# Sums of blocks for a seven-product layer: from subtractions on VectorE to additions in place, a part of them by adding DMA transfers

## The chip, the core and the metric

One core of a Trainium2 chip runs the whole program in one launch. The metric is device microseconds (us) of one execution; lower is better. The kernel before the change takes 979.97 us, the median of three runs (979.74 to 980.07).

## What is computed

Three layers follow one another: an attention whose weights are sigmoids, a two-matrix layer with `h * cos(h)` between its matrices (layer 1), and a two-matrix layer with a rational function between its matrices (layer 2).

```python
scores = scale * q @ k.T - log(S);  attn = 1 / (1 + exp(-scores));  x = attn @ v     # 4 x 12 heads, S = 448, D = 64
h = x @ w_in;  g = h * cos(h);  x = g @ w_out                                       # layer 1: 768 -> 2048 -> 768
h = x @ w_in2                                                                       # layer 2: 768 -> 2048 -> 768
P = a0 + a1*h + a2*h**2 + a3*h**3
Q = 1 + |b0|*|h| + |b1|*h**2
out = (P / (Q + 1e-6)) @ w_out2                                                     # 1792 tokens in all
```

## The kernel before

Every operand of layers 1 and 2 is split into two f16 halves (high and low), and a product is three matmuls: high by high, high by low, low by high. A split is two instructions: ScalarE writes the high half, VectorE subtracts it from the value and writes the low half.

Tokens come in four blocks of 448. Layer 2 takes them in two pairs (`pr` 0 and 1) and treats each of its two matrix products as a 2x2 block product with seven block products in place of eight (`NOP = 7`). For this it needs sums of blocks of the weights (made once, during layer 1) and sums of blocks of the activations (made for each pair), and it adds up the seven results in groups. The stages of layer 2, each once per pair:

- `y_nodes` (L1272) makes the seven activation operands of the first matrix, for each of three row groups `d`: four sums by `sub` (L1313 to 1319, VectorE, f32, 128x448), then the seven splits by `hl` (L1321). It begins when the largest value of layer 1's result is known (`sc`). For pair 1 the sums `t1`, `t2`, `t4` lie in new tiles and the three groups `d` run one after another (`gate`).
- `h2_nodes` (L1477) runs the first matrix: eight steps `k`, each with seven products of nine matmuls, in the order 0, 4, 5, 1, 6, 2, 3. Two PSUM tiles of two banks each, `xv` and `yw`, hold the results. Three small steps pass results between the banks: `seed` (L1513) and `save` (L1517) on ScalarE, and two additions of 128x448 on VectorE, `va` and `wa` (L1520). In each step `va` comes between products 1 and 6 and writes `xv`; `wa` follows product 6 and writes `yw`; product 2 follows `va`, product 3 follows `wa`.
- `item_nodes` (L1435) applies the rational function to the `xv` tile once product 2 is done and to the `yw` tile once product 3 is done: six VectorE instructions of 128x896 each (L110 and L1464) and five on ScalarE (L1449). The first product of the next step waits until the `xv` tile has been read for the last time (`xfree`), the seed until the `yw` tile has (`yfree`).
- `operand_nodes` (L1547) makes the seven operands of the second matrix for each of eight `k`: five sums (L1570 and L1585, VectorE, f32, 128x448) and seven splits (L1554, L1558). The splits are kept in one order over all products and `k` (`order_split`): product 0 for all `k`, then 5, 4, 2, 6, 3, 1.
- `o2_nodes` (L1594) runs the second matrix: seven products, each 24 units of three matmuls (eight `k`, three column groups `e`), and `end` (L1668) takes the banks out: a scaled copy on ScalarE (L1684) or a scaled addition on VectorE (L110, `wt<-o,ig,wt`), then the DMA to the output.

TensorE's order of stages is: first matrix of pair 0 (from about 528 us), the products 0, 5, 4, 2 of pair 0's second matrix (from 674.5 us), the first matrix of pair 1 (from 731.6 us) and then all seven products of pair 1's second matrix (from 875.6 us). Work of another stage is put between the products of a first matrix as filler: 96 units of layer 1 in pair 0, the 72 units of products 6, 3, 1 of pair 0's second matrix in pair 1. `FLOOR0` and `FLOOR1` say how many filler units must have run at each step.

The order on every engine is fixed when the program is built. `arrange` (L688) is a planner: each node has an engine, a duration and dependences, `LAT` holds the delays between engines, and the planner places one instruction after another; a filler unit is taken when the next product isn't ready in the plan. Each engine then runs its instructions in that order. GpSimd takes a few of the sums (`flex`). No DMA is issued from GpSimd; all but two come from SyncE's queue.

Of the kernel before, what the change touches and what calls it, by code (L numbers as in the profile page):

```python
# [10 lines left out]
F32 = mybir.dt.float32  # L11
# [12 lines left out]
def sigmoid_attention_moe_cos_moe_rational(  # L24
# [229 lines left out]
    with tc.manual_schedule():  # L254
# [336 lines left out]
        def l1_consts(bt):  # L591
            i = L1[bt][2]
            ck, iy = (col(f"{n}{bt}", tag=n, bufs=B) for n in ("ck", "iy"))
            ts(V, ck, i, 1.0 / (2.0 * math.pi))
            V.tensor_tensor(out=iy, in0=i, in1=irho, op=ALU.mult)
            return ck, iy
# [28 lines left out]
        g2s, n2s, rgs, wss, obs = (Slots("b", []) for _ in range(5))  # L625
# [18 lines left out]
        class Node:  # L644

            def __init__(self, eng, dur, fn, deps=(), acq=None, rel=None, due=None, soon=False, rush=False, lk=False, cov=False):
                self.eng, self.dur, self.fn = eng, dur, fn
                self.lk, self.cov, self.tied, self.flex, self.patience = lk, cov, False, False, PATIENT
# [11 lines left out]
        SOON, LAG, DMA, AHEAD, ALONE, PATIENT, LATER = 0.3, 0.5, 330.0, 8.0, 3.0, 4.0, 10.0  # L660
# [3 lines left out]
        def lat(a_, b_):  # L664
            return 0.0 if a_ in b_.weak else LAT.get((a_.eng, b_.eng), 0.1)
# [13 lines left out]

        kind = {"V": V.engine, "G": G.engine}  # L680
# [3 lines left out]

# [4 lines left out]
        def arrange(stock, groups, start):  # L689
            nominal = {}  # L690
            t = start
            for k, n in enumerate(pe):
                nominal[n] = t
                t += n.dur
                for g in groups:
                    if g["a"] <= k < g["b"]:
                        at = sorted(g["floors"].items()) + [(g["b"], len(g["units"]))]
                        i = max(i for i, (x, _) in enumerate(at) if x <= k)
                        (x0, n0), (x1, n1) = at[i:i + 2]
                        for u in g["units"][n0 + (n1 - n0) * (k - x0) // (x1 - x0):n0 + (n1 - n0) * (k + 1 - x0) // (x1 - x0)]:  # L700
                            t += u.dur
                            nominal[u] = t
# [63 lines left out]
            def commit(n, t):  # L766
# [3 lines left out]
                if n.lk or n.eng == "G":  # L770
# [13 lines left out]
            while len(queue) < total:  # L784
# [7 lines left out]
                if not cand:  # L792
# [3 lines left out]
                    for g, gr in enumerate(groups):  # L796
                        u = gr["units"]
                        if not u or pos < gr["a"]:
# [19 lines left out]
                for e in ("A", "V", "G", "D"):  # L818
# [3 lines left out]
                    if e == "G":  # L822
                        c = [(max(r, port[0], min(late[n] - ALONE, r + n.patience)), n) for r, n in c]
# [18 lines left out]
                if n.cov and now["G"] <= t + 0.05 and port[0] <= t + 0.05:  # L842
                    c = [m for m in avail["G"] + [m for m in avail["V"] if m.flex and m is not n] for r in (when(m),) if r is not None and r <= t + 0.3]
# [173 lines left out]
        def o1_end(bt, e, unit):  # L1017
            st = {}

            def copy():  # L1020
                r = st[0] = U([P, S], F32, f"yr{bt}_{e}")
                A.activation(out=r, in_=acc1[bt, e][:, :S], func=AF.Copy, scale=L1c[bt][1])
# [72 lines left out]
        s2i, i2i = col("s2i", NDH), col("i2i", ND)  # L1095
        s2o, i2o = (col(n, NFH) for n in ("s2o", "i2o"))
# [37 lines left out]
        def w2i_value_nodes(dues):  # L1134
# [20 lines left out]
            def fin():  # L1155
# [3 lines left out]
                V.tensor_copy(i2i[:, NDH:], i2i[:, :NDH])  # L1159

            scaled["i"] = N("V", 1.3, fin, ends, due=due)

        def w2i_nodes(dues, opened):
            done = []
            for n, (c0, w) in enumerate(W_S):
                stored_in[n] = []
                for rp in range(NDH):
# [19 lines left out]
                    def hl(x, op, deps, free=False, v=v, w=w, rp=rp, n=n, nm=nm, due=due):  # L1187
                        r = hl_nodes(
                            lambda: v[x], w, s2i[:, rp:rp + 1], ws_in[n][:, :, rp, op], [*deps, scaled["i"]],
# [20 lines left out]
        def w2o_nodes(dues):  # L1210
# [3 lines left out]
            for k in range(NFH):  # L1214
# [12 lines left out]
                def fin(k=k, c=c):  # L1227
                    m = col(f"m2p{k}", tag="mro", bufs=2)
                    V.tensor_tensor(out=m, in0=m2o[:, 2 * k:2 * k + 1], in1=m2o[:, 2 * k + 1:2 * k + 2], op=ALU.add)
                    sum_scale(m, s2o[:, c], i2o[:, c], f"2o{k}")  # L1230

# [13 lines left out]
                def hl(get, w, dst, deps, name, free=None, c=c, k=k, fn=fn, due=due):  # L1245
                    r = hl_nodes(
                        get, w, s2o[:, c], dst, [fn, *deps], f"h2o_{k}_{name}", "hl", hs,
# [6 lines left out]
                s1 = tt((2, 0), (0, 1), (1, 1), ALU.add, v3, {"v": 1})  # L1254
# [3 lines left out]
                hb = hl(lambda st=st: st[1]["v"], DM, ws_out[:, 2:4, k], [s1], "b")  # L1258
# [16 lines left out]
        def y_nodes(pr, tmp, drop, res, due, after=()):  # L1275
# [31 lines left out]
            for d in range(NDH):  # L1307
# [5 lines left out]
                def sub(o, i0, i1, deps, new, d=d, b=b, begin=begin, gate=gate):  # L1313
                    def f():
                        if not b:
                            begin()
                        if o not in b:
                            b[o] = tmp([P, S], f"yt{o}_{pr}_{d}")
                        V.tensor_tensor(out=b[o], in0=b[i0], in1=b[i1], op=ALU.subtract)  # L1319
                    return N("V", C448, f, [*gate, *deps], {res: 1} if new else {}, due=due, lk=True)  # L1320

                def hl(x, op, deps, rel, last_users=(), d=d, b=b, begin=begin, gate=gate):
# [6 lines left out]
                    def lo():  # L1329
                        t = tt2[pr, d, op]  # L1330
                        stt(V, t[:, 1, :], b[x], L2[pr][3][:, d:d + 1], t[:, 0, :], ALU.mult, ALU.subtract)
                        if rel and isinstance(x, int):
                            h_, i_ = ((0, 0), (1, 0), (1, 1), (0, 1))[x]
                            SU.drop(f"yr{b0 + i_}_{d + h_ * NDH}")
                        elif rel:
                            drop(f"yt{x}_{pr}_{d}")

                    h = N("A", A448 + PTR, hi, [*gate, *deps], {"u": 1}, due=due)
                    l = N("V", C448 + PTR, lo, [h, *last_users], rel=rel, due=due, lk=True)
                    tt_ready[pr, d, op] = l  # L1340
                    outs.append(l)
                    return h, l

                u1, r1 = {"u": 1}, {res: 1}
                t1 = sub("t1", 3, 0, [], True)
                hl(0, 0, [], u1, [t1])
                t3 = sub(3, 2, 3, [t1], False)
                hl(3, 6, [t3], u1)
                t2 = sub("t2", 2, "t1", [t1], True)
                hl(2, 2, [], u1, [t2, t3])  # L1350
                t4 = sub("t4", 1, "t2", [t2], True)
                hl(1, 1, [], u1, [t4])
                hl("t1", 4, [t1], r1, [t2])
                hl("t2", 5, [t2], r1, [t4])
                gate = [hl("t4", 3, [t4], r1)[1]]
# [46 lines left out]
        def l2_scale(pr):  # L1402
# [11 lines left out]
            ks = []  # L1414
            for n, x in enumerate((L2c[pr][1], ab[:, 2:3], ab[:, 1:2], L2c[pr][2])):
                ks.append(col(f"ks{n}{pr}", NFH))
# [430 lines left out]
```

## Time and profile before

| | |
|---|---|
| median of three runs | 979.97 us |
| profiled execution, own time | 979.13 us |
| its span, first to last instruction | 977.3 us |
| TensorE busy | 960.8 us (98%) |
| VectorE busy | 839.3 us (86%) |
| ScalarE busy | 612.9 us (63%) |
| GpSimd busy | 83.5 us (9%) |
| granted TensorE clock | 1.00 |
| share of the chain that ended last | PE 86%, DVE 12% |

The profile calls TensorE's matmuls PE, VectorE DVE, ScalarE ACT, GpSimd POOL and SyncE SP. Busy time is a mean over stages. A row of a timeline has the start, the length, the engine, the line, the operation, the tiles, and in brackets how long the engine was idle before it and which instruction ended that.

### The profile page before, as it was taken

The numbers are of one execution on the slowest core, as the hardware profiler recorded it, in microseconds if no ns is written. First come the engines' busy times: TensorE is split into PE (matmuls) and PEld (weight loads), VectorE is DVE, ScalarE is ACT, GpSimd is POOL, SyncE is SP. The second block draws the span as 40 slices with busy tenths as digits, with TensorE's granted clock in tenths as the row PEclk, the third lists the DMA queues.
The fourth block names the chain that finished last, engine by engine and source line by source line (L and its number), as shares of the span: only waits on it lengthen the run. The fifth ranks groups of instructions, "written<-read, shape, count | busy, mean of one in ns | idle before, by whom it ended". The sixth has DMA issues, their size and how long they took to land.

```text
span 977.3 us, 14073 instructions
## 1 busy us (share of the span) xinstructions
PE 960.8 (98%) x5255; PEld 486.8 (50%) x5255; DVE 839.3 (86%) x1282; ACT 612.9 (63%) x851; POOL 83.5 (9%) x85
## 2 busy tenths in 40 slices
PE   9999999999999999999999999999999999989998
PEld 4444445555555555555555555555454455444554
DVE  6999979999999879969995698888999999999901
ACT  7999976645755455645774576567685666567600
POOL 0000001220222011210222000001000001000000
PEclk9999999999999999999999999999999999999999
DMA  8788874446455766569612133122343334403353
GB/s 316 275 293 309 306 278 147 168 170 235 162 198 196 245 219 212 201 206 297 213 44 113 57 107 144 57 80 107 112 123 109 122 115 175 134 0 97 114 171 104
DMA packets 70964, 164.50 MB, mean 168 GB/s; under 512 B 6000, under 2 KB 44016, under 8 KB 68848
## 3 DMA queue, kind: packets, MB, share of 16 engines
q1 hardware_dynamic: 70608, 163.26, 49.4%
q8 instruction: 41, 0.67, 0.3%
q10 hardware_dynamic: 288, 0.34, 0.1%
q14 instruction: 27, 0.22, 0.1%
HBM read 129.76 MB, written 33.82 MB: 167 GB/s over the span
## 4 chain that ended last, share of the span: by engine, by line
PE 86%; DVE 12%; issue 1%; ACT 1%; DMA 0%; DVEq 0%; ACTq 0%
PE hx L584 22%; PE o L999 22%; PE o L1645 10%; PE xv L1429 10%; PE v L333 7%; PE yw L1429 7%; PE s L312 5%; DVE ua L1558 2%; DVE ba L110 2%; DVE ba L1570 1%; DVE w L110 1%; DVE ua L110 1%; PE s_None L307 1%; DVE rg L1558 1%; DVE ua L1319 1%
## 5 line engine op out<-in xcount | busy, mean ns | idle before, releaser
L999 PE MATMUL o<-ba,wo 128*128 128x448 f16 x1152 | 226.3, 352 | 0.0
L584 PE MATMUL hx<-ua,wi 128*128 128x448 f16 x1152 | 222.3, 352 | 0.0
L584 PEld LDWEIGHTS <-wi 128*128 128x128 f16 x1152 | 112.5, 98 | 106.1 <-issue 1.4
L999 PEld LDWEIGHTS <-wo 128*128 128x128 f16 x1152 | 112.6, 98 | 105.0
L1429 PEld LDWEIGHTS <-wi 128*128 128x128 f16 x1008 | 98.5, 98 | 99.0 <-issue 7.5
L1645 PEld LDWEIGHTS <-wt 128*128 128x128 f16 x1008 | 98.6, 98 | 98.1 <-issue 6.7
L1645 PE MATMUL o<-ua,wt 128*128 128x448 f16 x630 | 125.7, 352 | 3.0 <-ACT ua L1554 1.5
L1429 PE MATMUL xv<-ua,wi 128*128 128x448 f16 x576 | 117.0, 352 | 2.8 <-DVE ba L110 2.8
L958 POOL TENSOR_TENSOR ba<-ba 128x448 f16<-128x448 f32 x64 | 71.3, 1118 | 458.1 <-DVE ba L107 170.5
L1429 PE MATMUL yw<-ua,wi 128*128 128x448 f16 x432 | 89.5, 352 | 3.2 <-DVE xv L1520 2.1
L110 DVE SCALAR_TENSOR_TENSOR w<-w,u 128x896 f32<-128x896 f32 x64 | 69.0, 1087 | 14.7 <-ACT u L1449 14.1
L317 ACT ACTIVATE a<-s,nlogs 128x896 f32<-128x896 f32 x72 | 69.7, 1013 | 9.1 <-PE s L312 8.9
L110 DVE SCALAR_TENSOR_TENSOR ba<-ua,ba 128x768 int32<-128x768 int32 (+1 forms) x68 | 65.6, 971 | 0.2
L333 PE MATMUL v<-a,v 128*64 128x448 f32 x288 | 63.9, 554 | 0.0
L955 ACT ACTIVATE ba<-ba 128x896 f16<-128x896 f32 x32 | 30.4, 950 | 30.2 <-DVE ba L110 29.8
L1645 PE MATMUL o<-rg,wt 128*128 128x448 f16 x216 | 46.8, 352 | 2.2 <-ACT rg L1554 1.6
L944 ACT ACTIVATE ba<-ba,halfpi 128x896 f32<-128x896 f32 x32 | 33.3, 1040 | 23.1 <-DVE ba L110 22.6
L1449 ACT ACTIVATE ba<-xv,ks,ks 128x896 f32<-128x896 f32 x16 | 17.5, 1096 | 46.9 <-PE xv L1429 46.9
L110 DVE SCALAR_TENSOR_TENSOR wt<-o,ig,wt 128x448 f32<-128x448 f32 (+1 forms) x19 | 12.1, 655 | 40.4 <-PE o L1645 40.4
L1449 ACT ACTIVATE u<-w,c 128x896 f32<-128x896 f32 x32 | 33.2, 1037 | 19.4 <-DVE w L1464 19.4
L110 DVE SCALAR_TENSOR_TENSOR ba<-hx,ck,ba 128x896 f32<-128x896 f32 (+1 forms) x33 | 36.8, 1115 | 9.1 <-ACT ba L937 9.1
L937 ACT ACTIVATE ba<-hx,quarter,ck 128x896 int32<-128x896 f32 (+1 forms) x33 | 35.2, 1066 | 12.2 <-PE hx L584 12.1
(189 smaller groups left out, 1388.4 us busy)
## 6 DMA issues: line engine op xcount, KB each, us to landing
wi<-wsi SPq DMA_DIRECT2D x16, 1344.0 KB, 5.6
wt<-wso SPq DMA_DIRECT2D x56, 384.0 KB, 3.1
ua<-in_moe_w_out_dram SPq DMA_DIRECT2D x21, 768.0 KB, 4.2
p1o<-in_moe_w_out_dram SPq DMA_DIRECT2D x16, 768.0 KB, 6.0
wsi<-ua SPq DMA_DIRECT2D x42, 256.0 KB, 2.9
f1i<-in_moe_w_in_dram SPq DMA_DIRECT2D x12, 768.0 KB, 4.8
wso<-ba SPq DMA_DIRECT2D x24, 384.0 KB, 2.6
ba<-in_moe_w_out_dram SPq DMA_DIRECT2D x11, 768.0 KB, 4.3
```

The costliest lines, as they stand in the source:

```text
L110: eng.scalar_tensor_tensor(out=o, in0=i0, scalar=s, in1=i1, op0=op0, op1=op1)
L312: T.matmul(ps[:, h, :S], mqk[p, "k"][kl][r, c * P:c * P + P], mqk[p, "q"][ql][r], start=(i == 0), stop=(i == 2),)
L317: A.activation(out=t, in_=ps[:, :, :S], func=AF.Sigmoid, bias=cst["nlogs"], scale=QK)
L333: T.matmul(pvt[2 * o + j][h * D:(h + 1) * D, :S], vt[r, b * D:(b + 1) * D], at[r, h], start=c == (None if i else 0), stop=c == (NC - 1 if ...
L584: T.matmul(ps[:, :S], w[:, wl, f * P:(f + 1) * P], x[:, xl, :], start=(n == 0), stop=(n == 3 * ND - 1),)
L937: A.activation(out=o, in_=x, func=AF.Identity, scale=L1c[bt][0], bias=cst["quarter"])
L944: A.activation(out=st["r"], in_=st["r"], func=AF.Sin, scale=2.0 * math.pi, bias=cst["halfpi"])
L958: G.tensor_tensor(out=st["g"][:, j, 1, :], in0=st["r"][:, j], in1=st["g"][:, j, 0, :], op=ALU.subtract)
L999: T.matmul(acc1[bt, e][:, :S], w[:, wl, e * P:(e + 1) * P], g[:, gl, :], start=f == 0 and i == 0, stop=f == NF - 1 and i == 2,)
L1429: T.matmul(o[:, :S], w[:, d, op, wl, :], x[:, xl, :], start=start and n == 0, stop=n == 3 * NDH - 1, skip_group_check=not start,)
L1449: A.activation(out=st[o], in_=psv() if i_ == "ps" else st[i_], func=func, **{k: v() if callable(v) else v for k, v in kw.items()})
L1645: T.matmul(o[:, :S], w[:, k % 2, e, wl, :], g[:, gl, :], start=new and i == 0, stop=k == NFH - 1 and i == 2, skip_group_check=op not in FIRST,
```

## The change

In layer 2's activation sums every subtraction becomes an addition onto a block that is already there. For that, signs move into the constants: the scale of some weight products is negated (`NEGATIVE`, `n2i`, `n2o`), layer 1's result is scaled by `iy` or by `-iy` by block, the polynomial's constants exist in two signs, and the first two sums of each row group of the second weight matrix become `stt(-1 * a) op b`.

- The first matrix's four sums `t3`, `t1`, `t2`, `t4` are in place, in a chain where each needs the one before. In pair 0 they stay on VectorE, in pair 1 all twelve are DMA transfers that add (`YDMA`), issued from GpSimd. In pair 1 the three row groups no longer wait for one another.
- The second matrix's sums are four for each `k` in place of five. In pair 1, `t3`, `t1` and `t4` of the first six `k` are adding DMA transfers (`TDMA`), 18 in all.
- Products that need no sum (2, 1, 0) come first in the second matrix, then 5, 4, 6, 3. In pair 0, three products stand ahead of pair 1's first matrix and four (96 units) are its filler. Product 0 is now added and no longer copied, and product 4's bank is read twice.
- In the first matrix, `va` writes `yw` and no longer waits for product 1; product 2 goes to `yw` and waits for `wa`, which writes `xv`; the item on `xv` may begin after `wa`, ahead of products 2 and 3.

```diff
+        def summed(out_, in_, deps, due=None, dma=True):
+            if not dma:
+                n = N("V", C448, lambda: on(n).tensor_tensor(out=out_(), in0=out_(), in1=in_(), op=ALU.add), deps, due=due, lk=True)
+                n.flex = True
+                return n
+            n = N("G", ISSUE, lambda: G.dma_start(out=out_(), in_=in_(), accum_op=ALU.add), deps, due=due)
+            n.dma = True
+            return n
...
-        SOON, LAG, DMA, AHEAD, ALONE, PATIENT, LATER = 0.3, 0.5, 330.0, 8.0, 3.0, 4.0, 10.0
+        SOON, LAG, DMA, AHEAD, ALONE, PATIENT, LATER, ISSUE, LAND = 0.3, 0.5, 330.0, 8.0, 3.0, 4.0, 10.0, 0.95, 5.5
...
-                        V.tensor_tensor(out=half(*o), in0=half(*a_), in1=half(*b_), op=op)
+                        if o[0] == 2:
+                            stt(V, half(*o), half(*a_), -1.0, half(*b_), ALU.mult, op)
+                        else:
+                            V.tensor_tensor(out=half(*o), in0=half(*a_), in1=half(*b_), op=op)
...
+                h2 = hl(2, 2, [])
+                t3 = sub(2, 3, h2)
+                h0 = hl(0, 0, [])
+                t1 = sub(3, 0, [t3])
+                t2 = sub(0, 2, [t1, *h0])
+                h1 = hl(1, 1, [])
+                t4 = sub(1, 0, [t2, *h1])
+                hl(2, 6, [t3], True, [t2])
+                hl(3, 4, [t1], True)
+                hl(0, 5, [t2], True, [t4])
+                last = hl(1, 3, [t4], True)[1]
+                if gated:
+                    gate = [last]
...
-                va = N("V", C448, lambda add=add: add("x"), [p6, p2, saved], soon=True)
+                va = N("V", C448, lambda add=add: add("y"), [p6, saved, *yfree], soon=True)
                 p7 = pn(6, ("y", 0), False, [va])
-                wa = N("V", C448, lambda add=add: add("y"), [p7, saved, *yfree], None, {"s5": 1}, soon=True)
-                p3 = pn(2, ("x", 1), False, [va])
+                p3 = pn(2, ("y", 1), False, [va])
+                wa = N("V", C448, lambda add=add: add("x"), [p7, p2, saved], None, {"s5": 1}, soon=True)
+                p3.deps.append(wa)
+                wa.users.append(p3)
...
-                xfree = item_nodes(pr, k, lambda ps=ps: ps["x"], [p2, p3], ready, (p3, 16.0))
-                yfree = item_nodes(pr, k + NG, lambda ps=ps: ps["y"], [p4, wa], ready, (p4, 18.0))
+                xfree = item_nodes(pr, k, lambda ps=ps: ps["x"], [p2, wa], ready, (p7, 16.0))
+                yfree = item_nodes(pr, k + NG, lambda ps=ps: ps["y"], [p4, p3], ready, (p4, 18.0))
...
-        OPS = ((0, 5, 4, 2), (6, 3, 1)), ((0, 5, 4, 2, 6, 3, 1),)
+        OPS = ((2, 1, 0), (5, 4, 6, 3)), ((2, 1, 0, 5, 4, 6, 3),)
...
+                p3 = split(2, k, b22, [a_])
                 p1 = split(0, k, b11, [a_])
                 p2 = split(1, k, b21, [b_])
...
+                t3 = summed(b22, b12, [b_, *p3], dma=k < TDMA[pr][0])
+                t1 = summed(b12, b11, [t3], dma=k < TDMA[pr][1])
+                t2 = summed(b11, b22, [t1, *p1], dma=k < TDMA[pr][2])
+                t4 = summed(b21, b11, [t2, *p2], dma=k < TDMA[pr][3])
...
+            COPY = {2: "c12", 1: "c11", 5: "c21", 4: "c22"}
+            ADD = {4: ("c12", 0, 1), 6: ("c22", 1, 1), 3: ("c21", 1, 0), 0: ("c11", 0, 0)}
...
-        FLOOR1 = (0, 5, 14, 23, 32, 41, 50, 59)
+        YDMA, TDMA = (False, True), ((0, 0, 0, 0), (6, 6, 0, 6))
+        FLOOR1, KEEP1 = (0, 6, 20, 34, 48, 62, 76, 88), 0
```

In the names of the code, `p1`, `p5`, `p6`, `p2`, `p7`, `p3`, `p4` of `h2_nodes` are the products 0, 4, 5, 1, 6, 2, 3.

## Rows read from the trace of the kernel before

**Rows 1.** The page's first part: busy us, share of the span, instructions.

```profile
PE 960.8 (98%) x5255; PEld 486.8 (50%) x5255; DVE 839.3 (86%) x1282; ACT 612.9 (63%) x851; POOL 83.5 (9%) x85
```

**Rows 2.** Windows by stage: length, then busy us of PE, PEld, DVE, ACT, POOL.

```profile
528.00:674.50 146.50, 146.50 (x776) 75.74 (x775) 112.12 (x123) 85.68 (x102) 2.03 (x2) 1.00 0.24 88
674.50:731.40 56.90, 54.86 (x290) 28.23 (x289) 56.39 (x111) 42.77 (x75) 4.48 (x4) 1.00 0.41 126
731.40:848.00 116.60, 115.18 (x609) 59.41 (x608) 109.34 (x143) 72.34 (x92) 4.52 (x4) 1.00 0.38 131
848.00:875.50 27.50, 22.11 (x115) 11.03 (x114) 24.98 (x29) 17.12 (x22) 1.13 (x1) 1.00 0.13 40
875.50:925.00 49.50, 47.16 (x249) 24.14 (x247) 49.12 (x81) 35.71 (x64) 1.14 (x1) 1.00 0.32 96
925.00:977.30 52.30, 48.88 (x259) 25.06 (x257) 9.33 (x16) 3.74 (x7) 0.00 (x0) 1.00 0.43 136
```

**Rows 3.** Waits of PE, 674.5 to 925 us: total us, times, longest.

```profile
PE xv L1429 <- DVE ba L110: 2.8, 1, 2.8
PE yw L1429 <- DVE xv L1520: 2.1, 3, 0.7
PE o L1645 <- ACT rg L1554: 1.6, 1, 1.6
PE o L1645 <- ACT ua L1554: 1.5, 1, 1.5
```

**Rows 4.** Timeline, 841 to 866 us: fillers, the xv item, TensorE's waits.

```profile
841.16 3.57 PE L1645 MATMUL o<-ua,wt 128*128 128x448 f16 x18
...
853.40 1.86 PE L1429 MATMUL yw<-ua,wi 128*128 128x448 f16 x9 [0.72 <-DVE xv L1520]
...
857.00 1.10 ACT L1449 ACTIVATE ba<-xv,ks,ks 128x896 f32<-128x896 f32 x1 [1.99 <-PE xv L1429]
...
860.22 1.15 DVE L110 SCALAR_TENSOR_TENSOR ba<-ba,ks,xv 128x896 f32<-128x896 f32 x1
...
861.51 3.56 PE L1429 MATMUL xv<-ua,wi 128*128 128x448 f16 x18 [2.85 <-DVE ba L110]
...
866.17 1.86 PE L1429 MATMUL yw<-ua,wi 128*128 128x448 f16 x9 [1.09 <-ACT yw L1513]
```

**Rows 5.** Timeline, 875 to 888 us: the start of the last stage.

```profile
875.56 5.27 PE L1645 MATMUL o<-ua,wt 128*128 128x448 f16 x27
...
886.77 1.08 DVE L110 SCALAR_TENSOR_TENSOR w<-w,u 128x896 f32<-128x896 f32 x1
...
887.52 0.35 PE L1645 MATMUL o<-rg,wt 128*128 128x448 f16 x1 [1.58 <-ACT rg L1554]
```

**Rows 6.** VectorE by line and form: count, busy us, mean ns, idle before.

```profile
L1319 DVE TENSOR_TENSOR ua<-ua 128x448 f32<-128x448 f32 x10 | 6.1, 618 | 0.0
L1570 DVE TENSOR_TENSOR ba<-ba 128x448 f32<-128x448 f32 x16 | 9.6, 620 | 0.2
L110 DVE SCALAR_TENSOR_TENSOR wt<-o,ig,wt 128x448 f32<-128x448 f32 x9 | 5.8, 675 | 0.0
L1242 DVE TENSOR_TENSOR ba<-ba 128x384 f32<-128x384 f32 x32 | 19.0, 604 | 3.6 <-DMA wsv<-ba 3.1
L110 DVE SCALAR_TENSOR_TENSOR ba<-ba,s2o 128x384 f16<-128x384 f32 x8 | 4.9, 611 | 0.0
```

**Rows 7.** DMA issues, 680 to 780 us: count, KB each, median us to landing.

```profile
wt<-wso SPq DMA_DIRECT2D x20, 384.0 KB, 3.1
wi<-wsi SPq DMA_DIRECT2D x2, 1344.0 KB, 5.7
out_dram<-wt SPq DMA_DIRECT2D x5, 224.0 KB, 2.9
```

**Rows 8.** Timeline, 714 to 736 us: pair 1's first operand, products 0 and 4.

```profile
714.27 1.23 ACT L1327 ACTIVATE ua<-ua,kx_y 128x448 f16<-128x448 f32 x2 [0.63 <-DVE kx_y L105]
...
731.60 1.87 PE L1429 MATMUL xv<-ua,wi 128*128 128x448 f16 x9
...
735.57 1.87 PE L1429 MATMUL xv<-ua,wi 128*128 128x448 f16 x9
```

More of the change, by code (lines that the diff above doesn't have):

```diff
@@ L769, in commit @@
                 n.end = now[n.eng] = t + n.dur
-                if n.lk or n.eng == "G":
+                if n.lk or n.eng == "G" and not n.dma:
                     port[0] = n.end
@@ L822, in arrange @@
                     if e == "G":
-                        c = [(max(r, port[0], min(late[n] - ALONE, r + n.patience)), n) for r, n in c]
+                        c = [(r if n.dma else max(r, port[0], min(late[n] - ALONE, r + n.patience)), n) for r, n in c]
                     if not c:
@@ L1311, in begin, with sub, hl @@
                     b.update({k: yraw[b0 + i, d + h * NDH] for k, h, i in ((0, 0, 0), (1, 1, 0), (2, 1, 1), (3, 0, 1))})
[L1313 to L1322, printed above, removed]
+                def sub(o, i, deps, d=d, b=b, begin=begin):
+                    return summed(lambda: b[o], lambda: b[i], deps, due, YDMA[pr])
+                def hl(x, op, deps, rel=False, readers=(), d=d, b=b, begin=begin, gate=gate):
                     def hi():
@@ L1681, in run, with copy @@
-                def run():
-                    if not add:
+                rel = {"ps": 1} if op in FINAL else {}
+                dep = [u]
+                if op in COPY:
+                    dst = COPY[op]
+                    def copy(dst=dst):
                         obs.get(f"{dst}_{pr}_{e}")
                         A.activation(out=tile_(dst), in_=ps(), func=AF.Copy, scale=ig())
-                        return
-                    t = tile_(dst)
-                    if not tail:
-                        stt(V, t, ps(), ig(), t, ALU.mult, ALU.add)
-                        return
-                    w = S // 2
-                    for x, q_ in ((slice(0, w), SY), (slice(w, S), A)):
-                        stt(V, t[:, x], ps()[:, x], ig(), t[:, x], ALU.mult, ALU.add)
-                        q_.dma_start(out[r, c0 + x.start:c0 + x.stop], t[:, x])
@@ new lines, in end, with add @@
+                if op in ADD:
+                    dst, i, b = ADD[op]
+                    r = slice((i * NDH + e) * P, (i * NDH + e + 1) * P)
+                    c0 = (2 * pr + b) * S
+                    tail = last and op == ops[-1] and e == NDH - 1
+                    def add():
+                        t = tile_(dst)
+                        if not tail:
+                            stt(V, t, ps(), ig(), t, ALU.mult, ALU.add)
+                            return
+                        w = S // 2
+                        for x, q_ in ((slice(0, w), SY), (slice(w, S), A)):
+                            stt(V, t[:, x], ps()[:, x], ig(), t[:, x], ALU.mult, ALU.add)
+                            q_.dma_start(out[r, c0 + x.start:c0 + x.stop], t[:, x])
@@ L1785, in sigmoid_attention_moe_cos_moe_rational @@
         a0, b0_ = h2_nodes(0, [c0, c1], [pe[-1]])
-        groups = [{"a": a0, "b": b0_, "units": o1f, "floors": {a0 + 7 * k: n for k, n in enumerate(FLOOR0)}}]
+        groups = [{"a": a0, "b": b0_, "units": o1f, "floors": {a0 + 7 * k: n for k, n in enumerate(FLOOR0)}, "keep": KEEP0}]
         operand_nodes(0, [c0, c1])
@@ L1794, in sigmoid_attention_moe_cos_moe_rational @@
         a1, b1 = h2_nodes(1, [c0, c1], [])
-        groups.append({"a": a1, "b": b1, "units": o2f, "floors": {a1 + 7 * k: n for k, n in enumerate(FLOOR1)}})
+        groups.append({"a": a1, "b": b1, "units": o2f, "floors": {a1 + 7 * k: n for k, n in enumerate(FLOOR1)}, "keep": KEEP1})
         operand_nodes(1, [c0, c1])
```

159 lines of the change are left out of this document (63 added, 96 removed).

## The prediction, on record before the result

> **What bounds the kernel now.** I read the page's busy shares first, then windows by stage, then TensorE's waits, then the timeline around the longest of them. The shares make TensorE the bound: it is busy 960.8 of 977.3 us [rows 1], and the change takes away none of its products, so only its idle time, 16.5 us, can be won. The windows show where that lies [rows 2]. The first matrix of pair 0 has none. From 674.5 us on the stages have 2.04, 1.42, 5.39 and 2.34 us, 11.19 in all; the last window has 3.42 us, and what is left, 16.5 - 11.19 - 3.42 = 1.9 us, lies ahead of 528 us. Neither of these two does the change touch: the last matmul is followed by one scaled addition and one store as before, and the start is attention.
>
> In the three windows from 674.5 to 875.5 us VectorE is busy 56.39 + 109.34 + 24.98 = 190.7 of 201.0 us, while TensorE is busy 54.86 + 115.18 + 22.11 = 192.15 us. In pair 0's first matrix VectorE is busy only 112.1 of 146.5 us, and TensorE never waits there [rows 2]. So this stretch has two engines nearly full, and VectorE is the one that makes the other wait. TensorE's waits say the same: 2.8 us for the item on `xv`, 2.1 us in three pieces for `va`, 1.6 and 1.5 us for the high half of a split that itself stood behind the item's six VectorE steps [rows 3]. The timeline shows the two patterns. In the last steps of pair 1 filler is used up: after a block of six units at 841.16 us the gaps of 0.72, 2.85 and 1.09 us stand open [rows 4]. At the start of the last stage TensorE reaches `k` = 7 of its first product before that operand exists: the item ends with the instruction at 886.77 us, TensorE resumes at 887.52 us after 1.58 us, and then waits 0.6 us more for the low half [rows 5].
>
> **VectorE's work in that stretch.** Twelve sums of pair 1 leave VectorE: 12 x 6.1/10 = 7.3 us [rows 6]. Pair 0's second matrix needs four sums for each `k` and not five: 8 x 9.6/16 = 4.8 us [rows 6]. Product 0 is added where it was copied: three more scaled additions, 3 x 5.8/9 = 1.9 us [rows 6]; ScalarE's copies stay twelve, since product 4's bank is now copied and product 2's still is. The second set of polynomial constants is about five small column instructions; no row here is theirs, so 0 to 0.6 us each, and I take 0.2, 1 us in all. Net: 7.3 + 4.8 - 1.9 - 1.0 = 9.2 us less, so VectorE has 181.5 us. With the 10.3 us that it idles there now, that is 191.8 us, about TensorE's 192.15. If the two meet, all 2.04 + 1.42 + 5.39 = 8.85 us go. I take two thirds, 6.0 us: VectorE's idle time is made of waits for ScalarE inside the item's chain, and these don't shrink with its load. The lower end is 0, if filler still runs out in the last steps; the upper 8.85.
>
> **Order inside the first matrix.** `va` now runs beneath product 1, so the gap of 0.72 us ahead of product 6 closes; but product 2 now waits for `wa`, which opens a like gap ahead of it. I put this at nothing. The gain is the item's start: it may begin after `wa`, two products earlier, and nine matmuls take half of 3.56 us, so 3.4 us of head start once matmuls overlap. Now the bank is free 4.4 us after the item's first instruction begins (857.00 to 861.37 us), and TensorE needs six filler units or waits 2.85 us [rows 4]. The head start covers that, and so filler is saved at every step. This is what makes the 6.0 us come out; it is not added to it.
>
> **Start of the second matrix.** Product 2 comes first and needs the `xv` item too, but that item is 3.4 us earlier, less some 0.7 us for the gap at `wa`. Against 1.58 + 0.6 us of waiting (2.34 in the window) 2.7 us would do [rows 2, 5]; the `yw` item runs on VectorE beside it, so I take 1.6 of the 2.34 us. The same pattern at 686 us is inside the 2.04 us of the first window. In the last stage VectorE also loses 26 sums (18 to DMA, eight not needed), 15.6 us, and gains 1.9 us; it is 49.12 of 49.5 us busy there, but TensorE waits only at its start [rows 2], so this buys nothing by itself.
>
> **The transfers that add.** Thirty DMAs of 224 KB from GpSimd replace VectorE's sums. The 18 of the second matrix have a cover: products 2, 1, 0 need no sums and take 72 units, and 249 matmuls in 47.16 us make a unit of three 0.57 us, so 41 us [rows 2]. The twelve of pair 1's activations have less. The first split runs at 714.27 us, product 0 starts at 731.60 us and product 4 at 735.57 us [rows 8]. After the change product 4 needs two transfers one behind the other, product 5 three, product 3 four. By the plan in the code a transfer costs 0.95 us of issue and 5.5 us to land: 714.3 + 1.3 (a split) + 2 x 6.45 + 1.3 + 1.9 (the other two row groups) = 731.7 us for product 4, one hop more, about 739 us, for product 5, and 746 us for product 3. The first three products end at 674.5 + 72 x 0.57 = 715.5 us; until 732 us 29 units of the 96 are used, and 67 stay where 72 are now. With the filler saved at each step that is enough, so I cost the chain at nothing.
>
> No row shows a DMA issued from GpSimd or one that adds. The nearest are a store of the same 224 KB, 2.9 us to landing in this stretch, and a load of six times that, 5.7 us [rows 7]; an addition moves its target twice, so 2.9 to 2 x 5.7 = 11.4 us. I take a value near the row of the same size, and so not above the plan's 5.5: in a fixed order an early landing gains nothing, so the term is 0. Late, it costs three hops ahead of product 5: 3 us for each us beyond 5.5, up to 17.7 us. What waits: ScalarE's high-half split of `t1`, and behind it in ScalarE's queue the bank copies and the splits that filler needs; on GpSimd, behind an issue that waits for a split, the later transfers and the sums that GpSimd takes (4.48 + 4.52 + 1.13 us of them in the stretch [rows 2]).
>
> The Trainium skill, DMA: Bandwidth & Descriptors, section "Anatomy of one DMA — SWDGE (gpsimd) path", gives a GpSimd-issued transfer 2.0 us plus its bytes over 436 GB/s; for 224 KB that is an estimate of 2.5 us, by which the term is 0 too. A rule speaks against the change: the Trainium skill, SBUF — State Buffer, section "SBUF: two separate sides", says that GpSimd cannot write descriptors while VectorE holds the shared port in its two-port modes, with an example of 3100 in place of 620 ns; by that every hop would be 2.5 us longer. The same page, "Who interferes with whom", infers that `tensor_tensor` doesn't hold the writing side. VectorE is 99% busy in this stretch [rows 2], so the first would bite, and no row here decides between them.
>
> **Elsewhere.** Sixteen half-row sums of weights become `stt`: 604 ns now, 611 ns for an `stt` of the same width [rows 6]; 0.1 us in layer 1, where TensorE hardly idles. The price is at most that.
>
> **Sum.** 979.13 us of the profiled execution, less 6.0, less 1.6: 971.5 us. The median of the runs is 0.84 us above that execution, so 972.4 us.
>
> **Rivals.**
> *A: little of it arrives.* GpSimd's queue now holds transfers, so the sums that it takes today (10.13 us at some 1.14 us each, nine) fall back to VectorE, 9 x 0.6 = 5.4 us; the relief is 9.2 - 5.4 = 3.8 us and the filler spent ahead of pair 1 is missed at the end. For it: VectorE at 95%. Against it: the earlier item. The gain is 0 to 5 us, 2.5 in the middle: 977.5 us. Chance 0.22.
> *B: slower, by late landings.* If a transfer lands later than planned, product 5 of pair 1's first step waits three times the excess, with the order fixed and ScalarE's queue standing. It eats the 7.6 us at 5.5 + 2.5 = 8.0 us; at 9 us TensorE loses 10.5 us and the time is 972.4 + 10.5 = 982.9 us. For it: no row has this kind of transfer, and weight loads of 5.7 us run beside it [rows 7]. Against it: 2.9 us for the same bytes. Chance 0.18. The rule of the Trainium skill on descriptors is one way into it: 3 x 2.5 us less what lies below the plan.
> *C: all of it arrives.* Every one of the 11.19 us goes: 968.8 us. It is the end of the forecast's case.
>
> **How the numbers follow.** The forecast's case, a gain of 5 to 11.2 us, has 0.60: 968.8 to 975 us. Range 968.5 to 982.5 us: A whole, and B up to a landing near 9 us; it leaves out some 0.1. Two runs of this kernel can be told apart from 0.2%, 2 us. Faster by more: 0.60 plus 0.13 of A, 0.73; within: 0.09 of A and 0.02 of B, 0.11; slower: 0.16.
>
> **What would show it.** TensorE's idle time from 674.5 us to the last stage near 3 us and not 8.85; no wait of 2.85 us for `xv`; below 1 us at the start of the last stage; VectorE near 181 us in the stretch; transfers landing within 5.5 us. Wrong, if filler is used up before the last step again, if TensorE or ScalarE waits for a DMA around 730 to 746 us, or if GpSimd no longer takes sums.

## The result and the profile after

The changed kernel takes 968.43 us (median of four runs, 968.14 to 968.57) against 979.99 us (979.74 to 980.07): a ratio of 0.9882 [0.9865, 0.9899], 11.6 us less. The forecast was 7.6 us less, which that interval leaves out. The time lies 0.07 us below the low end of the range, 968.5; that is less than the runs differ among themselves. The profiled execution takes 968.57 us, its span is 966.8 us. The page's busy shares of the changed kernel answer to [rows 1]:

```profile
PE 959.6 (99%) x5256; PEld 486.4 (50%) x5256; DVE 823.8 (85%) x1265; ACT 615.0 (64%) x851; POOL 109.9 (11%) x115
```

Windows of the changed kernel, cut where those of [rows 2] are (length, then busy us of PE, PEld, DVE, ACT, POOL; granted clock, DMA share, GB/s):

```profile
0.00:528.00 528.00, 525.36 (x2964) 262.24 (x2965) 480.00 (x798) 356.14 (x494) 74.06 (x76) 1.00 0.65 219
528.00:674.50 146.50, 145.94 (x773) 75.37 (x772) 114.58 (x125) 87.83 (x102) 4.32 (x4) 1.00 0.25 90
674.50:731.40 56.90, 56.45 (x299) 29.08 (x298) 55.58 (x121) 41.76 (x73) 11.68 (x13) 1.00 0.67 169
731.40:848.00 116.60, 116.60 (x618) 60.28 (x617) 103.52 (x119) 80.54 (x103) 13.72 (x15) 1.00 0.50 147
848.00:875.50 27.50, 27.50 (x147) 14.23 (x146) 26.09 (x30) 17.88 (x21) 0.87 (x1) 1.00 0.38 99
875.50:925.00 49.50, 49.50 (x263) 25.59 (x262) 37.71 (x67) 28.93 (x58) 5.25 (x6) 1.00 0.60 154
925.00:966.80 41.80, 38.20 (x202) 19.57 (x200) 6.28 (x10) 1.90 (x3) 0.00 (x0) 1.00 0.42 125
```

From 731.4 to 925 us the profile has no idle time of TensorE at all. The whole difference of the spans can be added up from the two sets of windows:

| us | before | after |
|---|---|---|
| idle, first 528 us | 1.90 | 2.64 |
| idle, pair 0's first matrix | 0.00 | 0.56 |
| idle, 674.5 us to the last stage | 8.85 | 0.45 |
| idle, start of the last stage (to 925 us) | 2.34 | 0.00 |
| idle, last window | 3.42 | 3.60 |
| TensorE busy | 960.79 | 959.56 |

So 10.74 us went in the two places that the prediction names, 1.48 us came back elsewhere, and 1.23 us of busy time went with the pauses: 10.5 us of span. The median gained 1 us more than that, as the profiled execution of before was 0.86 us below its median and that of after is 0.14 us above; this 1 us is the spread of the runs and no work of the change.

TensorE's waits of the changed kernel from 528 us on are two, where [rows 3] has four groups and the `xv` item among them:

```profile
PE yw L1445 <- ACT yw L1529: 0.6, 1, 0.6
PE yw L1445 <- DVE xv L1536: 0.3, 1, 0.3
```

Its timeline shows where product 4 comes now (against 735.57 us in [rows 8]), the one short wait, and the last steps of pair 1, where [rows 4] has the open gaps; one row of ScalarE, at 862.32 us, is the start of the last `xv` item:

```profile
717.11 3.57 PE L1445 MATMUL xv<-ua,wi 128*128 128x448 f16 x18
720.51 0.73 PE L1641 MATMUL o<-rg,wt 128*128 128x448 f16 x3
...
729.80 3.56 PE L1445 MATMUL yw<-ua,wi 128*128 128x448 f16 x18 [0.33 <-DVE xv L1536]
...
851.24 3.57 PE L1445 MATMUL xv<-ua,wi 128*128 128x448 f16 x18
854.64 1.30 PE L1641 MATMUL o<-ua,wt 128*128 128x448 f16 x6
...
859.75 1.86 PE L1445 MATMUL yw<-ua,wi 128*128 128x448 f16 x9
...
862.32 1.01 ACT L1465 ACTIVATE u<-xv,i_y 128x896 f32<-128x896 f32 x1 [4.42 <-DVE xv L1536]
862.59 3.57 PE L1445 MATMUL yw<-ua,wi 128*128 128x448 f16 x18
866.00 2.43 PE L1641 MATMUL o<-ba,wt 128*128 128x448 f16 x12
868.26 0.73 PE L1641 MATMUL o<-rg,wt 128*128 128x448 f16 x3
```

Products 0 and 4 run in one block of 18 on `xv`, products 2 and 3 in another on `yw`, with no gap inside either. The row at 859.75 us is product 6, and the item starts 2.57 us after it begins; in the kernel before that took 3.60 us (853.40 and 857.00 us in [rows 4]). Three filler units are left behind the last product (the first nine matmuls of the twelve at 866.00 us), and the last stage follows without a wait. The DMA issues of the changed kernel (count, KB each, median us from issue to landing) show the adding transfers beside the plain store of the same size:

```profile
out_dram<-wt SPq DMA_DIRECT2D x23, 224.0 KB, 2.5
ba<-ba POOLq DMA_DIRECT2D x18, 224.0 KB, 5.1
ua<-ua POOLq DMA_DIRECT2D x12, 224.0 KB, 5.4
```

### The profile page after: what moved, and what is told of

The parts are those of the page before. It is cut to its first block, busy times and chain, and to the rows that moved or that the text cites. A ratio compares the mean times of both kernels' runs of the same rounds, so it can differ in the third digit from the quotient of the medians.

```text
span 966.8 us, 14097 instructions
## 1 busy us (share of the span) xinstructions
PE 959.6 (99%) x5256; PEld 486.4 (50%) x5256; DVE 823.8 (85%) x1265; ACT 615.0 (64%) x851; POOL 109.9 (11%) x115
## 4 chain that ended last, share of the span: by engine, by line
PE 94%; DVE 4%; ACT 1%; issue 0%; DMA 0%; DVEq 0%; ACTq 0%
PE hx L584 23%; PE o L1013 22%; PE o L1641 17%; PE yw L1445 11%; PE xv L1445 8%; PE v L333 7%; PE s L312 5%; PE s_None L307 1%; DVE ua L110 1%; DVE ua L1576 1%; DVE ba L684 0%; DMA k<-in_k_dram 0%; ACT u L1465 0%; DVE rg L1576 0%; DVE wt L110 0%
## 5 line engine op out<-in xcount | busy, mean ns | idle before, releaser
L1641 PE MATMUL o<-ua,wt 128*128 128x448 f16 x693 | 136.8, 352 | 0.0
L1445 PE MATMUL yw<-ua,wi 128*128 128x448 f16 x576 | 116.8, 352 | 1.0 <-ACT yw L1529 0.6
L1445 PE MATMUL xv<-ua,wi 128*128 128x448 f16 x432 | 87.0, 352 | 0.0
L110 DVE SCALAR_TENSOR_TENSOR wt<-o,ig,wt 128x448 f32<-128x448 f32 (+1 forms) x25 | 16.4, 662 | 44.5 <-ACT wt L1678 23.7
L1572 ACT ACTIVATE ua<-ba 128x448 f16<-128x448 f32 x77 | 39.5, 567 | 16.9 <-DVE ba L684 7.5
L1465 ACT ACTIVATE ba<-xv,kp,kp 128x896 f32<-128x896 f32 x16 | 17.5, 1095 | 50.0 <-DVE xv L1536 50.0
L110 DVE SCALAR_TENSOR_TENSOR ba<-ba 128x768 int32<-128x768 int32 (+2 forms) x48 | 40.7, 847 | 3.4 <-DMA wsv<-ba 2.6
L1576 DVE TENSOR_TENSOR ua<-ba,ua 128x448 f16<-128x448 f32 x74 | 42.2, 620 | 1.2 <-ACT ua L1572 1.1
```

Of the source, the lines that this page charges most:

```text
L110: eng.scalar_tensor_tensor(out=o, in0=i0, scalar=s, in1=i1, op0=op0, op1=op1)
L1445: T.matmul(o[:, :S], w[:, d, op, wl, :], x[:, xl, :], start=start and n == 0, stop=n == 3 * NDH - 1, skip_group_check=not start,)
L1572: A.activation(out=t[:, 0, :], in_=get(), func=AF.Copy)
L1576: on(l).tensor_tensor(out=t[:, 1, :], in0=get(), in1=t[:, 0, :], op=ALU.subtract)
L1641: T.matmul(o[:, :S], w[:, k % 2, e, wl, :], g[:, gl, :], start=new and i == 0, stop=k == NFH - 1 and i == 2, skip_group_check=op not in FIRST,
```

## Experiments

Each kernel is the changed one with one edit, where nothing else is said. They ran on several chips; the kernel before took 980.57 to 981.48 us (medians) beside them and 979.99 us in the first comparison, so differences of about 1 us between two prices say nothing. Two theories stood at first. *Relief*: VectorE's lighter load in the full stretch is what counts, above all the twelve sums of pair 1. *Head start*: it is the earlier start of the `xv` item.

**All thirty sums back on VectorE.**

```diff
-    YDMA, TDMA = (False, True), ((0, 0, 0, 0), (6, 6, 0, 6))
+    YDMA, TDMA = (False, False), ((0, 0, 0, 0), (0, 0, 0, 0))
```

> The changed kernel with all thirty sums back on VectorE (none by DMA); order, head start of the xv item and the filler of 96 units stay. Relief theory (VectorE's load decides): twelve sums, 7.3 us, return to the stretch from 674.5 us to the start of the last stage, and the time is 973 to 976 us. Head-start theory (the xv item's earlier start and the longer filler decide): TensorE's waits stay near 1 us and the time is 968.2 to 970 us.

Measured: 974.30 us, ratio 0.9933 [0.9912, 0.9954]; 5.9 us dearer than the changed kernel, as relief has it. The timeline of this kernel shows the place:

```profile
716.42 1.87 PE L1445 MATMUL xv<-ua,wi 128*128 128x448 f16 x9
...
717.92 3.30 DVE L684 TENSOR_TENSOR ua<-ua 128x448 f32<-128x448 f32 x6
...
721.13 0.68 DVE L110 SCALAR_TENSOR_TENSOR wt<-o,ig,wt 128x448 f32<-128x448 f32 x1
...
721.87 0.73 PE L1641 MATMUL o<-rg,wt 128*128 128x448 f16 x3 [3.58 <-DVE wt L110]
...
724.72 2.00 PE L1641 MATMUL o<-ua,wt 128*128 128x448 f16 x6
```

Six sums stand in VectorE's queue ahead of the addition that empties product 0's bank, and TensorE waits 3.58 us for that bank. Then its matmuls are slow: six take 2.00 us at 724.72, where six take 1.30 us in the changed kernel (854.64 above), and the granted clock of this kernel is below full in the windows around and after the wait (the number behind the five engines):

```profile
720.00:724.00 4.00, 1.96 (x8) 0.76 (x8) 4.00 (x8) 1.26 (x2) 0.00 (x0) 0.84 0.15 57
724.00:728.00 4.00, 4.00 (x17) 1.87 (x16) 3.83 (x20) 1.42 (x3) 0.00 (x0) 0.73 0.15 57
```

Of the span's 5.8 us more, 3.7 us are idle time of TensorE and 2.1 us busy time.

**Which of the thirty.** In one kernel only the twelve return (`YDMA` false for both pairs), in the other only the eighteen (`TDMA` all 0).

> Only the twelve sums of pair 1's first operands return to VectorE; the eighteen of the second matrix stay DMAs. Relief theory: the whole price of no_dma, 973 to 976 us, since these twelve are the ones in the full stretch. Head-start theory: 968.2 to 969.5 us.

> Only the eighteen sums of the second matrix return to VectorE, 10.8 us; they fall mostly in the last stage, where VectorE has some 12 us to spare in the 49.5 us window. Both theories: 968.2 to 969.5 us; above 971 us would say that the last stage needs the relief.

Measured: 975.00 us for the twelve, 0.9938 [0.9917, 0.9959]; 968.65 us for the eighteen, 0.9875 [0.9854, 0.9895]. The twelve carry the whole price, and TensorE's wait of 3.6 us for `wt` comes back with them. The eighteen transfers buy nothing that can be measured.

**Is it the order in the queue, or the load?** With all thirty on VectorE, product 0's additions are taken as soon as they can run, ahead of the sums.

```diff
-z = N("V", C448 + PTR, add, [*dep, acc2[dst, e]], None, rel, soon=True)
+z = N("V", C448 + PTR, add, [*dep, acc2[dst, e]], None, rel, soon=True, rush=op == 0)
```

> no_dma with one more thing: the planner takes the three scaled additions of product 0 as soon as they can run, ahead of the sums. In no_dma TensorE waited 4.4 us for them, 3.6 of it once, behind a block of six sums of pair 1, and the clock fell after it. Queue theory (the sums cost by standing ahead of one bank's release, not by their load): 968.5 to 971 us. Load theory (VectorE has no time for the twelve sums in this stretch): the wait moves and the time stays at 973 to 975 us.

Measured: 974.48 us, 0.9935 [0.9915, 0.9955]. The theory of the queue's order falls. TensorE's largest waits in this kernel (total us, times, longest):

```profile
PE yw L1445 <- ACT yw L1529: 2.0, 3, 0.8
PE o L1641 <- ACT wt L1678: 1.6, 1, 1.6
PE o L1641 <- DVE ua L1576: 1.3, 2, 0.8
```

The wait of 3.6 us is gone, the price is the same and lies in other waits. The other way round, the transfers stay and VectorE gets twelve useless additions of 128x448 ahead of pair 1's splits:

```diff
+def dummy(deps, op, d=d):
+    def f():
+        r = U([P, S], F32, f"ty{pr}_{d}_{op}")
+        V.tensor_tensor(out=r, in0=r, in1=r, op=ALU.add)
+    return N("V", C448, f, deps, {"u": 1}, due=due, lk=True)
...
```

> The changed kernel, its transfers kept, with twelve additions of 128x448 put on VectorE where the twelve sums of pair 1 would stand (they add a tile of no use to itself, ahead of the same splits): 7.3 us of load, no sum and no transfer changed. Load theory (VectorE's time in this stretch is what no_dma pays for): 973 to 976 us. Chain theory (it is the sums' place in the chain of splits, not VectorE's time): 968.4 to 970.5 us.

Measured: 975.61 us, 0.9943 [0.9928, 0.9958], where the changed kernel took 968.15 us (967.33 to 968.52) on the same chip. The additions cost 7.5 us, about one for one: VectorE is busy 7.0 us with the twelve. The splits of the sums stand behind them (ScalarE waited seven times for one, 8.7 us in all), so the kernel doesn't separate VectorE's time from a later start of these splits; it does show that the price comes without a change to any sum or transfer. TensorE's waits of this kernel from 840 to 880 us show that most of it is paid where filler ends, more than 120 us after the additions (703.6 to 729.0 us):

```profile
PE yw L1460 <- DVE xv L1551: 3.2, 2, 1.7
PE xv L1460 <- DVE ba L110: 0.9, 1, 0.9
PE yw L1460 <- ACT yw L1544: 0.8, 1, 0.8
```

How it gets there can be counted in the traces. These are the filler units that TensorE runs in each step of pair 1's first matrix, from one step's product 0 to the next's, and those left behind the last product:

| kernel | 1 | 2 | 3 | 4 | 5 | 6 | 7 | 8 | left |
|---|---|---|---|---|---|---|---|---|---|
| before (72 units) | 14 | 11 | 10 | 11 | 12 | 12 | 2 | 0 | 0 |
| changed (96 units) | 38 | 6 | 9 | 8 | 8 | 8 | 11 | 5 | 3 |
| with twelve useless additions | 55 | 6 | 8 | 8 | 8 | 8 | 3 | 0 | 0 |
| `xv` item planned late (next part) | 31 | 10 | 12 | 12 | 12 | 9 | 10 | 0 | 0 |

With the useless additions the first step takes 17 units more, and the last step has none. The changed kernel needs about 8 units in a step where the kernel before took 10 to 12.

**The head start taken out of the plan.** In the plan the `xv` item also waits for product 2 (and its due time is product 3's). The item doesn't read what product 2 writes.

```diff
-xfree = item_nodes(pr, k, lambda ps=ps: ps["x"], [p2, wa], ready, (p7, 16.0))
+xfree = item_nodes(pr, k, lambda ps=ps: ps["x"], [p2, wa, p3], ready, (p3, 16.0))
```

(In the code `p3` is the node of product 2, `p2` that of product 1.)

> The xv item may begin only when product 2 is done, as before the change (one more dependence in the plan, product 2's result is not used by it); DMAs stay. Head-start theory: the wait for the xv bank comes back or eats the filler, and 1 to 2 us return at the start of the last stage: 971 to 976 us. Relief theory: 968.5 to 970 us.

Measured: 978.84 us (ten runs, 977.93 to 979.65), 0.9981 [0.9971, 0.9991]. 10.4 us of the 11.6 are gone with the transfers in place. But the edit reaches only the plan. The timeline of this kernel in a step of pair 0:

```profile
576.75 1.87 PE L1445 MATMUL yw<-ua,wi 128*128 128x448 f16 x9
...
579.32 1.10 ACT L1465 ACTIVATE ba<-xv,kp,kp 128x896 f32<-128x896 f32 x1 [1.65 <-DVE xv L1536]
580.15 3.57 PE L1445 MATMUL yw<-ua,wi 128*128 128x448 f16 x18
```

On the chip the item starts 2.57 us after product 6 begins, as in the changed kernel, and ahead of product 2; in 12 of the 16 steps it is 2.6 to 2.8 us, and in none does it wait for product 2's end. What changed is the order: a plan that takes the bank to be free later puts more filler into a step (12 units in steps 3 to 5 in the table, where the changed kernel has 8 or 9), and none is left for the last one. So the price comes by the order and the filler that it spends, not by a later start of the item. TensorE's waits of this kernel from 674.5 to 900 us:

```profile
PE o L1641 <- ACT ua L1572: 3.7, 2, 2.3
PE yw L1445 <- DVE xv L1536: 1.3, 1, 1.3
PE yw L1445 <- ACT yw L1529: 1.3, 1, 1.3
PE o L1641 <- DVE ua L1576: 1.0, 2, 0.6
```

The largest stand at the starts of the second matrix, whose product 2 needs this item and ahead of which no filler is left; the timeline of this kernel at the first of them, and the window around it:

```profile
688.77 0.45 PE L1641 MATMUL o<-ua,wt 128*128 128x448 f16 x1 [2.33 <-ACT ua L1572]
689.64 0.90 PE L1641 MATMUL o<-ua,wt 128*128 128x448 f16 x2 [0.41 <-DVE ua L1576]
690.34 2.27 PE L1641 MATMUL o<-rg,wt 128*128 128x448 f16 x6
```

```profile
688.00:692.00 4.00, 2.81 (x8) 1.08 (x8) 4.00 (x7) 3.54 (x8) 0.00 (x0) 0.61 0.00 0
```

So relief holds, and of the head start what the plan makes of it; a kernel with both edits says whether they overlap:

> late_item and no_dma together: the xv item waits for product 2 and all sums are on VectorE. If the two effects add (10.4 and 5.9 us above 968.4): 984 to 986 us, slower than before. If they stand for the same missing time: 979 to 981 us, no more than late_item.

Measured: 987.66 us (987.59 to 989.95), 1.0073 [1.0049, 1.0098]. Together they cost 19.2 us, more than their sum (5.9 + 10.4 = 16.3 us), and what is left of the change is slower than the kernel before.

**The old order inside the first matrix**, as near as it can be had: `va` writes `xv` after product 1, product 2 follows `va`, the item on `xv` waits for product 2, the one on `yw` for `wa`. The blocks of the second matrix are named to match (not printed here); the signs that this order would need are left out, and the work is the same.

```diff
-va = N("V", C448, lambda add=add: add("y"), [p6, saved, *yfree], soon=True)
+va = N("V", C448, lambda add=add: add("x"), [p6, p2, saved], soon=True)
...
-    p3 = pn(2, ("y", 1), False, [va])
+    p3 = pn(2, ("x", 1), False, [va])
...
-xfree = item_nodes(pr, k, lambda ps=ps: ps["x"], [p2, wa], ready, (p7, 16.0))
-yfree = item_nodes(pr, k + NG, lambda ps=ps: ps["y"], [p4, p3], ready, (p4, 18.0))
+xfree = item_nodes(pr, k, lambda ps=ps: ps["x"], [p2, p3], ready, (p3, 16.0))
+yfree = item_nodes(pr, k + NG, lambda ps=ps: ps["y"], [p4, wa], ready, (p4, 18.0))
...
```

> The first matrix's inner order as before the change: va writes xv, wa writes yw, product 2 goes to xv and waits for va, the xv item waits for product 2; product 2 of the second matrix then needs the yw item. The signs of two blocks are wrong in it, so its output is not the reference's; transfers, in-place sums and the order of products stay. Head-start theory: most of the gain goes, 975 to 981 us, a little less than or like late_item (978.8). If late_item lost by a gap of its own (product 2 behind wa and the item behind product 2): 970 to 974 us.

> pair_undo with all sums on VectorE: what is left of the change is the order of products, the four sums in place of five and the longer filler. Its output is not the reference's, as in pair_undo. If these by themselves gain: below 979 us. If they cost unless the other two parts stand beside them: 982 to 990 us.

Measured: 985.91 us with the transfers, 1.0044 [1.0027, 1.0060], and 994.76 us without, 1.0139 [1.0124, 1.0154]. Both are dearer than expected. TensorE's largest wait in the first of them is again at the starts of the second matrix:

```profile
PE o L1639 <- ACT ua L1570: 7.3, 2, 4.2
```

Here the item does start later on the chip: 3.6 us after product 6 begins, as in the kernel before, and a step takes 9 to 13 units again (steps 2 to 7). But product 2 of the second matrix now needs the `yw` item, the later of the two, where it needs the `xv` item in the changed kernel. Two things were taken away at once, and the run can't price the head start by itself. It does show that with the old order inside a step the rest of the change is a loss.

**The landing time in the plan.** The planner's 5.5 us becomes 2.5 us in one kernel and 8.5 us in the other. Work and transfers are the same; only the fixed order changes. This tests rival B.

```diff
-... LATER, ISSUE, LAND = ... 10.0, 0.95, 5.5
+... LATER, ISSUE, LAND = ... 10.0, 0.95, 2.5
```

> The plan believes that a transfer lands in 2.5 us and not 5.5; the chip needs 5.1 to 5.4 as before, so every instruction placed behind a transfer comes up to 2.9 us too early in its queue. Price of the prediction's rival B (three hops in a row reach TensorE): 3 x 2.9 = 8.7 us, 975 to 978 us. Cover theory (the chain is through long before pair 1's first product): 968.3 to 970 us.

> The plan believes 8.5 us to landing. An early landing gains nothing and a cautious plan only moves the chain forward: 968 to 970 us by both; above 971 us would say that the plan's estimate has a price on this side too.

Measured: 976.95 us at 2.5, 0.9961 [0.9945, 0.9977]; 969.49 us at 8.5, 0.9883 [0.9861, 0.9905]. The timeline of the kernel planned with 2.5 us:

```profile
724.37 0.67 ACT L1341 ACTIVATE ua<-ua,kx_y 128x448 f16<-128x448 f32 x1 [1.66 <-DMA ua<-ua]
...
728.21 0.53 ACT L1529 ACTIVATE yw<-xv 128x448 f32<-128x448 f32 x1
...
728.79 3.52 PE L1445 MATMUL yw<-ua,wi 128*128 128x448 f16 x9 [7.12 <-ACT yw L1529]
```

ScalarE waits for a landing in its high-half splits, the seed of the step stands behind them, and TensorE waits 7.12 us for the seed. That is rival B's path. Its price came near, three hops of 5.4 - 2.5 = 2.9 us being 8.7 us and 8.5 us measured, but in part by luck: the wait itself is 7.12 us, and the nine matmuls behind it took 1.65 us longer than nine take elsewhere (1.87 us).

The kernel planned with 8.5 us has the changed kernel's ratio (0.9883 and 0.9882).

## Why the prediction was right or wrong

The direction and both places were right. The failing step is a size, and it is one sentence: "I take two thirds, 6.0 us". The stretch gave back 8.40 of its 8.85 us. The reason given for the discount, VectorE's waits inside the item's chain, cost TensorE next to nothing: VectorE idles 15.8 us in the three windows from 674.5 to 875.5 us, more than the 10.3 us of before, and TensorE 0.45 us, since it has another product or filler while that chain runs. By its own steps:

- **VectorE's work, 9.2 us less.** From 674.5 us to the start of the last stage, now at about 867 us and not 875.5, VectorE is busy 177.1 us, 13.6 us less. The relief was needed: returning the twelve sums costs 5.9 to 6.6 us, the same load as useless additions 7.5 us. Over the whole execution VectorE lost 15.5 us, where the terms for this stretch and for the last stage make 22.9. From 674.5 us on it is 20.0 us less, and ten sums that GpSimd no longer takes, against five low halves that it takes now, make some 3.1 us of the difference; ahead of 674.5 us VectorE is busy 4.5 us longer, which was not followed up.
- **The head start, "two products earlier", 3.4 us.** Mis-sized: before, the item waited for product 2 and not for product 3, and now it waits for `wa`, which follows product 6 as product 2 did. It starts 1.0 us earlier after product 6 (2.57 us and not 3.60). The filler that this order saves is what the prediction said of it, and more: two units and not six stand between a step's last product and the next step's first in most steps, and a plan that doesn't count on it loses 10.4 us. So as a condition of the 6.0 us it was right, and it was a stronger one than a discount of a third allows for.
- **Start of the second matrix, 1.6 us of 2.34.** All of it came. The item now starts 3.7 us ahead of the end of the last product and not 1.5, and three filler units (1.7 us) stand behind that product, which the working doesn't have; that part was luck. A row was misread there too: the item of before ends not with the instruction at 886.77 us but with this one, ahead of it.

```profile
885.71 1.15 DVE L110 SCALAR_TENSOR_TENSOR ba<-ba,ks,w 128x896 f32<-128x896 f32 x1
```

- **The y chain at nothing.** Right in its result, wrong in its steps. The working put product 4 at 732 us with 29 filler units spent ahead of pair 1; the planner starts the chain of scaling and sums 23 us earlier (the largest value is gathered at 689.25 us and not at 712.25), issues the transfers from 694.0 to 715.0 us, and product 4 runs at 717.11 us as second half of a block of 18. No unit was spent ahead. The value taken for the landing, near 2.9 us, was wrong for this place too: 5.4 us were measured, near the plan's 5.5, and 6.8 at most. It did no harm because the order was planned with 5.5 us and the chain began early.
- **The eighteen transfers and sums of the last stage at nothing:** right, 968.65 us without them.
- **Rival A** fell. GpSimd's sums did fall back in part, from nine in the stretch to five low halves, and no time was lost by it.
- **Rival B** didn't happen; its mechanism did, at about its price, as soon as the plan was told a landing that was too early.
- **Rival C** is what happened, nearly: 10.74 of its 11.19 us went in the profile. Its 968.8 us, on which the range's low end stands, was no floor. One reason is the 1 us of spread between medians and profiled executions. The other is "only its idle time, 16.5 us, can be won": idle time was read as span less busy time, but a matmul's modelled end counts as busy when nothing follows: the row of 18 matmuls at 717.11 us is 3.57 us long, and the next begins after 3.40. Each pause of before hid about 0.17 us so, and with the pauses gone TensorE is busy 1.23 us less with one instruction more. The profile lists 13 waits of TensorE over the whole execution before and 5 after; eight fewer would make 1.36 us.

Two rules of the Trainium skill were weighed ahead. By the Trainium skill, SBUF — State Buffer, section "SBUF: two separate sides", GpSimd can't write descriptors while VectorE runs in a two-port mode. Here the twelve issues took 0.88 us in the median and 1.54 at most with VectorE 98% busy, and the quickest of the eighteen landed in 3.0 to 3.1 us with VectorE 87% busy or more, so VectorE did not hold these up; whether its instructions here run in such a mode no run shows. By the Trainium skill, DMA: Bandwidth & Descriptors, section "Anatomy of one DMA — SWDGE (gpsimd) path", 224 KB are an estimate of 2.5 us. The quickest landings are not far from that; the medians of 5.1 and 5.4 us decide for a plan, and one that believed 2.5 us lost 8.5 us.

Open: what the item's earlier start on the chip is worth without the plan's use of it; what the longer filler (96 units and not 72) and the new order of the second matrix's products are worth by themselves (neither was tried with the rest of the change kept); and what each condition would bring alone in the kernel before; all prices here are those of taking a part out of the changed kernel.

## What to carry to other kernels

Where two engines are both nearly full and a third set of work serves as filler, a microsecond taken from the second engine was worth about one of the first here (5.9 to 7.5 us for twelve sums of 7 us), until the filler lasts to the end, and it is paid or saved far from where it was spent; count the filler units by step and look for the place where they run out. When a gain has two conditions, price each by taking it out alone, and look in the trace whether the edit took it out on the chip or only in the plan. A planner with fixed order should be told a landing time on the late side: 3 us too late cost nothing clear of the noise here, 3 us too early 8.5 us.

## What the runs showed of the hardware

An adding DMA of 224 KB issued from GpSimd took 5.1 to 5.4 us to landing in the median (3.6 to 6.8 for the twelve), twice the 2.5 us of a plain store of the same size in the same kernel. Most of the difference is not the addition. The twelve follow one another closely, with the DMA engines at a share of 1.00 from 694.0 to 715.5 us; plain loads of 384 KB took 5.2 us there and 3.3 over the whole execution. Of the eighteen, the quickest took 3.0 to 3.1 us. Two of them, from issue to landing, the first quick and the second the slowest that had GpSimd's queue to itself (length, busy us of the five engines, clock, DMA share, GB/s):

```profile
797.03:800.10 3.07, 3.07 (x18) 1.58 (x17) 2.67 (x3) 2.33 (x3) 0.86 (x1) 1.00 0.42 75
817.06:824.15 7.09, 7.09 (x39) 3.66 (x38) 6.46 (x8) 6.18 (x8) 0.87 (x1) 1.00 0.91 296
```

The packets of the trace say where the time went: the first packet moved 1.43 us after the issue in the quick one and 4.41 us after it in the slow one, while other transfers kept the DMA engines 97% busy. The adding transfers also cost more time of these engines: by the page of the changed kernel they (the second row) took 1.9 times as much of it for each byte as the queue that does most of the rest (packets, MB, share of the engines' time). Packets of the same 1792 bytes took 159 ns in the median in the adding transfers and 74 ns in the others; what of this is the addition and what is GpSimd's queue wasn't separated.

```profile
q1 hardware_dynamic: 70608, 163.26, 50.6%
q0 software_dynamic: 4320, 6.88, 4.1%
```

The granted clock fell after some of TensorE's waits, towards the lower of its levels: to 0.84 and 0.73 in the two windows of 4 us around and after the wait of 3.58 us, to 0.61 with waits of 2.33 and 0.41 us at 688.77 us, and to 0.50, that is 1.2 GHz throughout, in the window in which the wait of 7.12 us ends:

```profile
728.00:732.00 4.00, 3.21 (x9) 1.32 (x9) 2.35 (x4) 2.68 (x6) 0.00 (x0) 0.50 0.01 2
```

There nine matmuls took 3.52 us in place of 1.87. In the kernel before, the waits of 2.85 and 1.58 us left the clock at 1.00 in the windows around them [rows 2, 4, 5], and so did the waits of up to 1.7 us with the useless additions. What tells the two kinds apart was not tried.
